# Where a block of background steps stands among the units of a Fourier and gated feed-forward kernel: fixed spacing, or beside named units

## The chip, the cores and the metric

The kernel runs on one core of a Trainium2 chip. The metric is the device time of one execution in microseconds (us); before the change it was 1040.99 us, the median of 3 runs (1040.63 to 1042.91). The engines of a core, as the profile names them, are PE (matrix products, with PEld for its weight loads), DVE (elementwise work on vectors), ACT (elementwise work and copies), POOL (here mostly an issuer of DMAs) and SP (an issuer of DMAs). Each runs its own queue in order and waits on semaphores of the others.

## The reference, cut to what matters

```python
xn = _layernorm(x, axis=-1)                       # x: 2048 tokens of 640
a = xn @ dft_hid_re.T;  b = xn @ dft_hid_im.T
y = dft_seq_re @ a - dft_seq_im @ b               # 2048 x 2048 by 2048 x 640, twice
gate = xn @ W_gate;  up = xn @ W_up               # 640 x 1728 each
h = (gate * (gate > 0)) * up
return x + y + h @ W_down
```

All of it is in float32. The sequence matrices are the largest operand (two of 2048 x 2048).

## The kernel before, in words

**Products.** PE multiplies fp32r tiles here. To keep float32's precision an operand is split into a high part (ACT copies it to fp32r) and a low part (DVE subtracts the high part from the operand), and each product is three matmuls: high by high, high by low, low by high (`mm3`, lines 130 to 132; `split`, lines 124 and 125). On top of it products of 2 x 2 blocks are made with seven block products in place of eight, whose operands are sums and differences of blocks.

**Three phases.** The first phase multiplies the transposed sequence matrices with the layer-normalised tokens, in four chunks of 512 output positions (`NCHUNK`). The second makes gate and up and their product (`gate_up`); the third makes the hidden transform, the down projection and the sum (`project`).

**The first phase.** The block products are named B11, B21 (made first, for all four chunks), T1, T2, B22, T3 and T4. For each chunk come the units of the last five: four units (g = 0 to 3) per product, in the order T1 0 to 3, T2 0, B22 0, T2 1, B22 1, T2 2, T2 3, B22 2, B22 3, T3 0 to 3, T4 0 to 3. A unit has up to four steps (`stream`): it loads a tile of the sequence matrices on SP (`raw`, and for T1 also `tk`, 512 KB each, line 650); `prepare` subtracts on DVE where the product needs a difference (line 646) and splits the result into one of the three buffers of `cb` (lines 124, 125); `run` issues 18 matmuls for T1 and B22 and 12 for the others; the last unit of a product adds its result to the sums (`combine`, tiles `sa` and `sb`, lines 533, 536, 628), which POOL stores to `pq` (line 619). At T2 0 SP loads `sa` anew (line 667), which waits until the last store of `sa` has gone.

**The order of the work.** `drive(4, 2)` walks over the list `todo`: at place i it loads unit i, prepares unit i-2, runs unit i-4. It runs work that `defer` has put off to this place first. The framework's scheduler may then still move instructions in each engine's queue of this phase; `in_turn` lets a unit's preparation be issued only behind the third last low part, and `keep_in_program_order` holds a single instruction where it stands.

**The background steps.** The second phase needs the same sums of blocks of the normalised tokens, transposed, split in two parts and stored in DRAM (`sets`, `halves`). For one half of the tokens this is made during the first phase, in six steps (`token_sets`, `SET_STEPS`). Steps 0 and 1 each make half of one set: they load the mean and scale of 512 tokens, spread over the partitions, and a tile of the transposed input (POOL, lines 360, 361), add and multiply on DVE (364, 365), split, and store two DMAs. Steps 2 to 5 each make a quarter of the other eight sets: they load four DMAs (378, 379), add and multiply twice (384, 385), make four differences (391), split two tiles of 1024 columns, and store four DMAs (line 422). All of it lies in one tile, named `r` in the profile, with eight spots of 1024 columns that are used in turn. Before the change a step is one more entry of `todo`: its place is two entries behind V3 (the last of the `sums_3` entries in chunk 0), and then every nine entries (`SPACE`). `begin` issues the loads there, and all further work of the step at two places, 6 and 7 entries later (`halve`: the arithmetic and the split), and the stores 8 and 9 entries later (`keep`).

When the sets are stored, SP loads them into the tiles of the second phase during the last chunk (`load_halves`, line 721).

Of the kernel before, what the change touches and what calls it, by code (L numbers as in the profile page):

```python
# [8 lines left out]
F32R = mybir.dt.float32r  # L9
# [17 lines left out]
SET_STEPS = 6  # L27
# [31 lines left out]
def fnet_reglu_kernel(  # L59
# [15 lines left out]
    nc = tc.nc  # L75
# [47 lines left out]
    def split(hi, lo, src):  # L123
        nc.scalar.activation(hi, src, AF.Copy)  # L124
        return nc.vector.tensor_tensor(lo, src, hi.bitcast(F32), op=OP.subtract)  # L125
# [19 lines left out]
    todo = []  # L145
# [192 lines left out]
    def token_sets(q, step, place=None, unit=None):  # L338

        def work():  # L340
            if "work" not in late:
                late["work"] = get_r1(F32)
            i = late["places"] = (late.get("places", -1) + 1) % 8
            return late["work"][:, i * W2 : (i + 1) * W2]

        stage = place or work

        ch = xt[:, q * W2 : (q + 1) * W2].rearrange("(k p) t -> k p t", p=P)
        st_r = rows[:, q * W2 : (q + 1) * W2]
        tt = nc.vector.tensor_tensor  # L350
        part = lambda st, i: st[:, i * CH : (i + 1) * CH]
        t = {}

        if step < 2:
            cs = slice(step * CH, (step + 1) * CH)

            def load():
                t["mr"], t["a"] = stage(), stage()[:, :CH]
                for i in range(2):
                    nc.gpsimd.dma_start(part(t["mr"], i), st_r[i : i + 1, cs].to_broadcast([P, CH]))  # L360
                nc.gpsimd.dma_start(t["a"], ch[4][:, cs])

            def make():
                tc.keep_in_program_order(tt(t["a"], t["a"], part(t["mr"], 0), op=OP.add))
                tt(t["a"], t["a"], part(t["mr"], 1), op=OP.mult)

            made = [([make], "a", lambda v: halves[X4][:, v, cs], lambda ap: ap)]
            keep_whole = lambda: nc.gpsimd.dma_start(sets[X4][:, cs], t["a"])
        else:
            k, hs = (step - 2) // 2, (step - 2) % 2 * HC  # L370
            hs = slice(hs, hs + HC)
            cols = lambda ap: ap.rearrange("p (c t) -> p c t", c=2)
            cs = slice(k * CH + hs.start, k * CH + hs.stop)

            def load():
                t["mr"], t["ab"] = stage(), stage()
                for i in range(2):
                    nc.gpsimd.dma_start(cols(part(t["mr"], i)), cols(st_r[i : i + 1])[:, :, hs].to_broadcast([P, 2, HC]))
                    nc.gpsimd.dma_start(cols(part(t["ab"], i)), cols(ch[k + 2 * i])[:, :, hs])

            def make():
                mr, ab = t["mr"], t["ab"]
                for i in range(2):
                    tc.keep_in_program_order(tt(part(ab, i), part(ab, i), part(mr, 0), op=OP.add))  # L384
                    tt(part(ab, i), part(ab, i), part(mr, 1), op=OP.mult)

            def more():

                mr, ab = t["mr"], t["ab"]
                (a0, a1, b0, b1), (t1, t2, t3, t4) = ([st[:, i * HC : (i + 1) * HC] for i in range(4)] for st in (ab, mr))  # L390
                sub = lambda o, i0, i1: tt(o, i0, i1, op=OP.subtract)  # L391
                sub(t1, a1, a0)
                sub(t2, b1, t1)
                sub(t3, b1, a1)
                sub(t4, b0, t2)

            by_set = lambda ap: ap.rearrange("p (i t) -> p i t", i=4)
            made = [([make, more], "ab", lambda v: halves[B11 : B11 + 4, :, v, cs].rearrange("i p t -> p i t"), by_set),
                    ([], "mr", lambda v: halves[T1 : T1 + 4, :, v, cs].rearrange("i p t -> p i t"), by_set)]

            def keep_whole():
                for i, st in ((B11, t["ab"]), (T1, t["mr"])):
                    nc.gpsimd.dma_start(sets[i : i + 4, :, cs].rearrange("i p t -> p i t"), by_set(st))

        if unit:
            unit(load, made[0][0], keep_whole)
            return

        def begin():
            load()  # L410
            for i, (make, name, place, view) in enumerate(made):

                def halve(make=make, name=name):
                    for m in make:
                        m()
                    src = t[name]
                    t["h" + name] = h = work()[:, : src.shape[1]]
                    split(h.bitcast(F32R), src.bitcast(F32R), src)

                def keep(name=name, place=place, view=view):  # L420
                    for v, part in enumerate((t["h" + name], t[name])):
                        nc.gpsimd.dma_start(place(v), view(part))

                defer(6 + i, halve)
                defer(8 + i, keep)

        todo.append((begin, idle, idle, idle))

    def raw():
        return raw_p.tile([P, W2], F32, name="raw")  # L430
# [213 lines left out]
    def stream(c, name, g):  # L644
        t = {}
        sub = lambda o, i0, i1: nc.vector.tensor_tensor(o, i0, i1, op=OP.subtract)  # L646

        def get(m, half, o=None):
            o = raw() if o is None else o
            late["dma"] = nc.sync.dma_start(o, dft[c, m, half * NH + g]).ins  # L650
            return o

        def load():
            if name == "T1":
                t["s"] = get(0, 0)
                TK[g] = get(1, 0, tk.tile([P, W2], F32, name="tk"))
            elif name == "T2":
                ST[g] = get(1, 1)
            elif name == "T3":
                t["s"] = get(0, 0)  # L660
            elif name == "T4":
                t["s"] = get(0, 1)

        def prepare():
            if name == "T2" and g == 0:
                F["a"] = sums_a()
                nc.sync.dma_start(F["a"], firsts[c])
            src = t.get("s", TK[g])
            with in_turn():
                if name == "T1":  # L670
                    src = TK[g]
                    sub(src, src, t["s"])
                elif name == "T2":
                    sub(src, ST[g], src)
                elif name == "B22":
                    src = ST[g]
                elif name == "T3":
                    sub(src, TK[g], src)
                elif name == "T4":

                    sub(src, src, TK[g])
                t["b"] = b = parts()
                lows.append(split(flat(b, 0), flat(b, 1), src))

        def run():
            b = t["b"]
            es = lambda n: [(n, 0), (n, 1)]
            if name == "T1":
                product(g, b, resident(g, 2), es("e2"), True, False, ("v2", 0, True))
            elif name == "T2":  # L690
                product(g, b, resident(g, 0), es("e1"), True, False)
            elif name == "B22":
                product(g, b, fourth(g), es("e2"), False, True, ("v2", 1, False))
            elif name == "T3":
                product(g, b, resident(g + NH, 0), es("e1"), False, True)
            else:
                product(g, b, resident(g + NH, 2), es("e2"), True, False)

        todo.append((load, prepare, run, lambda: combine(c, name) if g == NH - 1 else None))
# [37 lines left out]
                f()  # L737
        todo.clear()

    steps = [(q, i) for q in (1,) for i in range(SET_STEPS)]  # L740
    early_sets, first_sets = list(SETS_A), list(SETS_B)
    free = [None]
    SPACE = 9

    def phase(c, names):


        for n in names.split():
# [9 lines left out]
                first_stream(int(n[3]), n[:3], int(n[4]))  # L758
            else:
                stream(c, n[:-1], int(n[-1]))  # L760
            if n == "V3":
                free[0] = len(todo) + 2
            if free[0] is not None and len(todo) >= free[0] and steps:
                token_sets(*steps.pop(0))
                free[0] = len(todo) + SPACE

    for n in ("B11", "B21"):
        for g in range(NH):
# [2 lines left out]
    phase(0, "V1 T10 T11 V2 T12 T13 V3 T20 B220 T21 B221 T22 T23 B222 B223 T30 T31 T32 T33 T40 T41 T42 T43")  # L771
    for c in range(1, NCHUNK - 1):
        phase(c, "T10 T11 T12 T13 T20 B220 T21 B221 T22 T23 B222 B223 T30 T31 T32 T33 T40 T41 T42 T43")
    assert not steps, len(steps)
    phase(NCHUNK - 1, "T10 T11 T12 T13 T20 B220 T21 B221 T22 T23 K K K A A B222 B223 T30 A T31 A T32 A T33 T40 T41 T42 T43 K")
    assert not early_sets and not first_sets
    drive(4, 2)
    ph1.close()


# [520 lines left out]
```

## Time and profile before

| | |
|---|---|
| median of 3 runs | 1040.99 us (1040.63 to 1042.91) |
| the profiled execution | 1040.59 us |
| its span on the core | 1038.7 us |
| PE busy | 1025.0 us, 99% of the span |
| DVE busy | 801.3 us, 77% |
| ACT busy | 432.1 us, 42% |
| POOL busy | 106.9 us, 10% |
| moved by DMA | 242.73 MB, mean 234 GB/s |

A row of a group or of the timeline names the line of the kernel, the engine, the operation and its tiles, out first: `cb<-raw` writes `cb` from `raw`. In the timeline the first two numbers are the start from the span's start and the duration in us; several equal instructions in a row are merged (x2), and the bracket gives the engine's idle time ahead and what ended it. In a row of windows the numbers after the stretch are PE, PEld, DVE, ACT and POOL busy in us, each with its count of instructions, then PE's granted clock as a share of full speed, the DMA engines' busy share and GB/s. In a row of waits stand who waited, for whom, the total in us, how many times, and the longest. The record of a matmul of 512 columns lasts 0.39 us while the next starts 0.23 us after it, so PE can lose time that its busy sum does not show: the starts tell it.

### The profile page before, as it was taken

How to read it: one execution, taken by the hardware profiler on the slowest of the kernel's cores; microseconds unless marked ns; L12 is line 12 of the kernel's file. 1: busy time of each engine (PE TensorE's matmuls, PEld its weight loads, DVE VectorE, ACT ScalarE, POOL GpSimd, SP SyncE). 2: the span in 40 equal slices, each digit the busy share in tenths (PEclk: the TensorE clock that was granted, in tenths of full speed). 3: DMA queues.
4: the chain of work that ended last, by engine and by line, in shares of the span. 5: the costliest groups of instructions: out<-in, count | busy, mean ns of one | idle time of the engine just before them, and what ended most of it. 6: DMA issues, size and time to landing. Idle time of an engine off the chain costs nothing.

```text
span 1038.7 us, 12463 instructions
## 1 busy us (share of the span) xinstructions
PE 1025.0 (99%) x4528; PEld 844.2 (81%) x4528; DVE 801.3 (77%) x1074; ACT 432.1 (42%) x544; POOL 106.9 (10%) x172
## 2 busy tenths in 40 slices
PE   9899999999999999999999999999999999999998
PEld 7788888888787888888888888888878888888886
DVE  7857887979979767688887988887498667786764
ACT  6654453333343423333334534433365423552521
POOL 3211000102121001321110010010000000000000
PEclk9999999999999999999999999999999999999999
DMA  8987743947977975763363666663698636986554
GB/s 303 320 284 258 255 141 115 333 171 251 364 239 273 391 304 190 250 237 136 149 233 135 225 223 237 229 248 122 207 367 292 197 120 217 379 299 219 159 157 122
DMA packets 101468, 242.73 MB, mean 234 GB/s; under 512 B 11552, under 2 KB 50976, under 8 KB 98848
## 3 DMA queue, kind: packets, MB, share of 16 engines
q1 hardware_dynamic: 83664, 171.68, 48.2%
q0 software_dynamic: 17744, 70.26, 18.4%
q8 instruction: 35, 0.57, 0.2%
q14 instruction: 25, 0.20, 0.1%
HBM read 182.12 MB, written 58.74 MB: 232 GB/s over the span
## 4 chain that ended last, share of the span: by engine, by line
PE 91%; DVE 5%; DMA 1%; ACT 1%; issue 1%; SPq 0%; DVEq 0%; ACTq 0%
PE ps L132 30%; PE ps L131 30%; PE ps L130 30%; DVE cb L125 1%; PE ps L1198 1%; PE ps L495 1%; DMA rw<-hd 1%; DVE raw L646 1%; DMA raw<-in_dft 1%; DVE r L125 0%; DVE tk L646 0%; ACT cb L124 0%; DVE bs L204 0%; DVE r L391 0%; DVE r L384 0%
## 5 line engine op out<-in xcount | busy, mean ns | idle before, releaser
L130 PE MATMUL ps<-cb,wt 128*128 128x512 f32 x390 | 151.9, 390 | 0.4 <-ACT wt L124 0.4
L132 PE MATMUL ps<-cb,wt 128*128 128x512 f32 x390 | 151.9, 390 | 0.4 <-DVE wt L125 0.4
L131 PE MATMUL ps<-cb,wt 128*128 128x512 f32 x390 | 151.8, 389 | 0.0
L125 DVE TENSOR_TENSOR cb<-rw,cb 128x1024 fp32r<-128x1024 f32 x83 | 94.1, 1134 | 69.3 <-ACT cb L124 68.7
L124 ACT ACTIVATE cb<-rw 128x1024 fp32r<-128x1024 f32 x83 | 81.9, 987 | 149.9 <-PE ps L132 124.8
L124 ACT ACTIVATE cb<-raw 128x1024 fp32r<-128x1024 f32 x75 | 79.4, 1060 | 132.1 <-PE ps L132 101.6
L125 DVE TENSOR_TENSOR cb<-raw,cb 128x1024 fp32r<-128x1024 f32 x75 | 91.5, 1223 | 42.0 <-ACT cb L124 41.8
L130 PE MATMUL ps<-cb,xs_late 128*128 128x512 f32 x256 | 99.3, 390 | 4.3 <-ACT xs_late L121 2.8
L131 PE MATMUL ps<-cb,xs_late 128*128 128x512 f32 x256 | 100.1, 391 | 1.4 <-DVE cb L125 1.2
L131 PE MATMUL ps<-xs_early,gw 128*128 128x512 f32 x260 | 101.2, 389 | 0.0
L130 PE MATMUL ps<-xs_early,gw 128*128 128x512 f32 x260 | 101.2, 389 | 0.0
L132 PE MATMUL ps<-xs_early,gw 128*128 128x512 f32 x260 | 101.1, 389 | 0.0
L132 PE MATMUL ps<-cb,xs_late 128*128 128x512 f32 x256 | 99.3, 389 | 0.0
L121 ACT ACTIVATE gw<-z 128x1024 fp32r<-128x1024 f32 (+1 forms) x52 | 57.6, 1110 | 77.7 <-DVE z L808 75.1
L132 PE MATMUL ps<-cb,xs_early 128*128 128x512 f32 x226 | 87.9, 389 | 0.0
L131 PE MATMUL ps<-cb,xs_early 128*128 128x512 f32 x226 | 87.9, 389 | 0.0
L130 PE MATMUL ps<-cb,xs_early 128*128 128x512 f32 x226 | 87.4, 390 | 0.4 <-ACT cb L124 0.4
L130 PEld LDWEIGHTS ps<-cb,wt 128*128 128x128 f32 x390 | 73.2, 188 | 16.1 <-ACT wt L124 0.9
L132 PEld LDWEIGHTS ps<-cb,wt 128*128 128x128 f32 x390 | 73.2, 188 | 15.9 <-DVE wt L125 0.7
L131 PEld LDWEIGHTS ps<-cb,wt 128*128 128x128 f32 x390 | 73.2, 188 | 15.7 <-DVE cb L125 0.3
L121 ACT ACTIVATE u<-ps 128x512 f32<-128x512 f32 x52 | 31.1, 599 | 93.7 <-PE ps L132 93.7
L818 DVE TENSOR_TENSOR gw<-z,gw 128x1024 fp32r<-128x1024 f32 (+1 forms) x52 | 64.7, 1286 | 3.8 <-ACT gw L121 3.8
(198 smaller groups left out, 1947.7 us busy)
## 6 DMA issues: line engine op xcount, KB each, us to landing
raw<-in_dft SPq DMA_DIRECT2D x94, 512.0 KB, 6.2
wt<-wparts SPq DMA_DIRECT2D x66, 256.0 KB, 3.2
z<-in_wgu SPq DMA_DIRECT2D x26, 640.0 KB, 3.9
hd<-ob POOLq DMA_DIRECT2D x26, 512.0 KB, 3.7
rw<-hd SPq DMA_DIRECT2D x24, 512.0 KB, 6.8
wparts<-pw POOLq DMA_DIRECT2D x11, 1024.0 KB, 4.1
tk<-in_dft SPq DMA_DIRECT2D x16, 512.0 KB, 7.0
set<-r POOLq DMA_DIRECT2D x16, 512.0 KB, 4.6
```

The lines of the kernel that those rows point to most:

```text
L121: return nc.scalar.activation(o, i, AF.Copy)
L124: nc.scalar.activation(hi, src, AF.Copy)
L125: return nc.vector.tensor_tensor(lo, src, hi.bitcast(F32), op=OP.subtract)
L130: nc.tensor.matmul(ps, wh, mh, start=first, stop=False, skip_group_check=more)
L131: nc.tensor.matmul(ps, wh, ml, start=False, stop=False, skip_group_check=more)
L132: nc.tensor.matmul(ps, wl, mh, start=False, stop=last, skip_group_check=more)
L495: start["pe"] = pin([nc.tensor.matmul(E[0, key], xn_part(n * SG + j, d)[v == 1], b[:, int(v == 2), j], start=False, stop=n == NH - 1 and ( ...
L646: sub = lambda o, i0, i1: nc.vector.tensor_tensor(o, i0, i1, op=OP.subtract)
L818: tt(self.w[:, 1, cs], self.z[:, cs], self.w[:, 0, cs].bitcast(F32), op=OP.subtract)
L1198: nc.tensor.matmul(B[key], wr[:, v, es], hr[:, cs], start=False, stop=v == 1, skip_group_check=not new)
```

## The change

A step is no longer an entry of `todo`. `token_sets` returns its load, its arithmetic and its splits as functions, and a table `hooks` puts each beside a unit: `stream`'s `prepare` runs what is entered for its chunk, product and g right after its own split. Steps 0 and 1 stand in chunk 0: loads beside T1 2 and T1 3, everything else beside B22 0 and B22 1. Steps 2 and 3 stand in chunk 1, steps 4 and 5 in chunk 2, all in the same way: loads a chunk ahead beside T3 3 and T4 1; of the arithmetic one half (an add and a multiply) beside each of T1 0 and T1 1 for the first step, T1 2 and T1 3 for the second; the four differences of the first step beside B22 0, its two splits beside B22 1; the differences and the first split of the second step beside B22 2, its second split beside B22 3. Stores follow two entries behind the split. The last of the six steps therefore ends in chunk 2, and `todo` has six entries fewer.

```diff
-            def make():
+            def make(two=range(2)):
                 mr, ab = t["mr"], t["ab"]
-                for i in range(2):
+                for i in two:
                     tc.keep_in_program_order(tt(part(ab, i), part(ab, i), part(mr, 0), op=OP.add))
                     tt(part(ab, i), part(ab, i), part(mr, 1), op=OP.mult)
...
-        def begin():
-            load()
-            for i, (make, name, place, view) in enumerate(made):
-
-                def halve(make=make, name=name):
-                    for m in make:
-                        m()
-                    src = t[name]
-                    t["h" + name] = h = work()[:, : src.shape[1]]
-                    split(h.bitcast(F32R), src.bitcast(F32R), src)
-
-                def keep(name=name, place=place, view=view):
-                    for v, part in enumerate((t["h" + name], t[name])):
-                        nc.gpsimd.dma_start(place(v), view(part))
-
-                defer(6 + i, halve)
-                defer(8 + i, keep)
-
-        todo.append((begin, idle, idle, idle))
+        def halve(name):
+            src = t[name]
+            t["h" + name] = h = work()[:, : src.shape[1]]
+            split(h.bitcast(F32R), src.bitcast(F32R), src)
+
+        def keep(name, place, view):
+            for v, part in enumerate((t["h" + name], t[name])):
+                nc.gpsimd.dma_start(place(v), view(part))
+
+        halves_of = {name: lambda name=name, place=place, view=view: (halve(name), defer(2, lambda: keep(name, place, view)))
+                     for _, name, place, view in made}
+        return load, made[0][0], halves_of
...
                 lows.append(split(flat(b, 0), flat(b, 1), src))
+            for f in hooks.pop((c, name, g), ()):
+                f()
...
-    steps = [(q, i) for q in (1,) for i in range(SET_STEPS)]
     early_sets, first_sets = list(SETS_A), list(SETS_B)
-    free = [None]
-    SPACE = 9
+    hooks = {}
+
+    def at(c, name, g, *fs):
+        hooks.setdefault((c, name, g), []).extend(fs)
+
+    for step in range(2):
+        load, make, halve = token_sets(1, step)
+        at(0, "T1", 2 + step, load)
+        at(0, "B22", step, *make, halve["a"])
+    for step in range(2, SET_STEPS):
+        load, (make, more), halve = token_sets(1, step)
+        c, i = 1 + (step - 2) // 2, step % 2
+        at(c - 1, *(("T3", 3), ("T4", 1))[i], load)
+        for j in range(2):
+            at(c, "T1", 2 * i + j, lambda make=make, j=j: make((j,)))
+        at(c, "B22", 2 * i, more, *([halve["ab"]] if i else []))
+        at(c, "B22", 2 * i + 1, *([halve["mr"]] if i else halve.values()))
...
-            if n == "V3":
-                free[0] = len(todo) + 2
-            if free[0] is not None and len(todo) >= free[0] and steps:
-                token_sets(*steps.pop(0))
-                free[0] = len(todo) + SPACE
```

More of the change, by code (lines that the diff above doesn't have):

```diff
@@ L773, in fnet_reglu_kernel @@
         phase(c, "T10 T11 T12 T13 T20 B220 T21 B221 T22 T23 B222 B223 T30 T31 T32 T33 T40 T41 T42 T43")
-    assert not steps, len(steps)
     phase(NCHUNK - 1, "T10 T11 T12 T13 T20 B220 T21 B221 T22 T23 K K K A A B222 B223 T30 A T31 A T32 A T33 T40 T41 T42 T43 K")
@@ L777, in fnet_reglu_kernel @@
     drive(4, 2)
+    assert not hooks
     ph1.close()
```

## The prediction

> **What bounds the kernel now.** I read the page first (share of each engine, clock), then the windows by stage, then PE's own timeline at the places where a window is not full, then the queue that PE waited for there. The windows are the four chunks of the first phase from the T1 products on: 142 to 207 us is chunk 0, then chunks 1, 2 and 3.
>
> ```profile
> PE 1025.0 (99%) x4528; PEld 844.2 (81%) x4528; DVE 801.3 (77%) x1074; ACT 432.1 (42%) x544; POOL 106.9 (10%) x172
> ...
> 142.00:207.00 65.00, 65.00 (x288) 53.85 (x287) 52.70 (x57) 25.32 (x27) 6.57 (x11) 1.00 0.58 198
> 207.00:275.00 68.00, 66.05 (x289) 53.70 (x289) 59.71 (x68) 26.46 (x26) 9.12 (x13) 1.00 0.68 245
> 275.00:343.00 68.00, 66.70 (x291) 54.04 (x290) 60.60 (x68) 26.13 (x26) 13.23 (x19) 1.00 0.79 282
> 343.00:408.00 65.00, 65.00 (x288) 53.84 (x287) 46.39 (x47) 22.00 (x22) 2.17 (x4) 1.00 0.81 311
> ```
>
> PE bounds the kernel, at the full granted clock (1.00 in each window). Chunks 0 and 3 run 288 matmuls in 65 us, 0.226 us each. Chunks 1 and 2 run 289 and 291 in 68 us, which at that pace are 65.2 and 65.7 us: 2.8 and 2.3 us are lost, 5.1 in all, though the busy column shows only 1.95 and 1.30 idle, because a record lasts 0.39 us and overlaps the next. So whatever rearranges VectorE (DVE) work in this phase can win at most about 5 us. PE's timeline shows where they go:
>
> ```profile
> 269.40 0.39 PE L132 MATMUL ps<-cb,xs_late 128*128 128x512 f32 x1
> 271.20 0.73 PE L130 MATMUL ps<-cb,xs_late 128*128 128x512 f32 x2 [1.41 <-ACT cb L124]
> 272.34 0.97 PE L130 MATMUL ps<-cb,xs_early 128*128 128x512 f32 x3 [0.41 <-ACT cb L124]
> 273.44 0.50 PE L131 MATMUL ps<-cb,xs_late 128*128 128x512 f32 x1
> 273.77 0.39 PE L132 MATMUL ps<-cb,xs_late 128*128 128x512 f32 x1
> ...
> 329.48 0.39 PE L132 MATMUL ps<-cb,xs_late 128*128 128x512 f32 x1
> 329.90 0.73 PE L130 MATMUL ps<-cb,xs_late 128*128 128x512 f32 x2
> 331.85 0.50 PE L131 MATMUL ps<-cb,xs_late 128*128 128x512 f32 x1 [1.22 <-DVE cb L125]
> ...
> 340.14 0.87 PE L130 MATMUL ps<-cb,xs_early 128*128 128x512 f32 x3
> 341.06 0.50 PE L131 MATMUL ps<-cb,xs_late 128*128 128x512 f32 x1
> ```
>
> From 269.40 to 273.77 seven matmuls start in 4.37 us where 7 x 0.227 = 1.59 would do: 2.78 lost. From 329.48 to 331.85 three start in 2.37: 1.69 lost. From 340.14 to 341.06 three start in 0.92: 0.24 lost. A restart costs about 0.1 more (273.77 comes 0.33 after 273.44), which the two later places pay too. That makes 4.9 us by the starts and 5.1 by the windows; I take 5.0. PE waited for the high (ACT) and low (DVE) part of a `cb` tile. In DVE's queue the reason stands just ahead:
>
> ```profile
> 255.79 0.69 DVE L384 TENSOR_TENSOR r<-r 128x512 f32<-128x512 f32 x1
> ...
> 260.47 1.09 DVE L391 TENSOR_TENSOR r<-r 128x256 f32<-128x256 f32 x3
> 261.47 1.23 DVE L125 TENSOR_TENSOR cb<-raw,cb 128x1024 fp32r<-128x1024 f32 x1
> ...
> 264.08 2.36 DVE L125 TENSOR_TENSOR r<-r 128x1024 fp32r<-128x1024 f32 x2
> 266.35 1.29 DVE L533 TENSOR_TENSOR sa<-ps,sa 128x512 f32<-128x512 f32 x2
> 267.55 1.29 DVE L536 SCALAR_TENSOR_TENSOR sb<-sb,sa 128x512 f32<-128x512 f32 x2
> 268.75 1.23 DVE L646 TENSOR_TENSOR raw<-raw,tk 128x1024 f32<-128x1024 f32 x1
> 269.88 2.36 DVE L646 TENSOR_TENSOR tk<-tk,raw 128x1024 f32<-128x1024 f32 x2
> 272.15 1.23 DVE L125 TENSOR_TENSOR cb<-raw,cb 128x1024 fp32r<-128x1024 f32 x1
> ```
>
> One whole token step (L384, L385, L391 and the two low parts of `r`) runs between 255.79 and 266.35, in T4, then the sums of T3. Only at 268.75 does the subtraction for T4's last unit come, while PE runs dry at 269.40. The same in chunk 2: the low parts of `r` at 323.76, and three low parts of `cb` late and in a heap at 330.57.
>
> ```profile
> 323.76 2.36 DVE L125 TENSOR_TENSOR r<-r 128x1024 fp32r<-128x1024 f32 x2
> ...
> 330.57 3.50 DVE L125 TENSOR_TENSOR cb<-raw,cb 128x1024 fp32r<-128x1024 f32 x3
> ```
>
> **The change part by part.** The amount of work stays: the listing of the two built programs has the same number of instructions on every engine (1076 on DVE, 546 on ACT, 177 on POOL, 439 on SP). So the sum has no term for work, only for position. In a row, an operation of 1024 columns takes 1.14 us of the queue (268.75 to 269.88), one of 512 columns 0.60 (266.35 to 267.55, two of them), one of 256 columns 0.33 (260.47 to 261.47, three). A step of the larger kind (2 to 5) is then 4 x 0.60 + 4 x 0.33 + 2 x 1.14 = 6.0 us of DVE, one of the smaller (0 and 1) 2 x 0.60 + 0.60 = 1.8.
>
> Load by chunk: chunk 3, which has no step, keeps DVE busy 46.4 of 65 us. With two steps, chunks 1 and 2 come to 58.4 of 65.3, so there is room for them. What matters is whether a low part is ever later than PE wants it. The measure is how far ahead DVE can be:
>
> ```profile
> 397.44 1.06 ACT L124 ACTIVATE cb<-raw 128x1024 fp32r<-128x1024 f32 x1 [1.66 <-PE ps L132]
> 400.15 1.06 ACT L124 ACTIVATE cb<-raw 128x1024 fp32r<-128x1024 f32 x1 [1.66 <-PE ps L132]
> ...
> 398.75 1.22 DVE L125 TENSOR_TENSOR cb<-raw,cb 128x1024 fp32r<-128x1024 f32 x1
> ...
> 401.25 1.23 DVE L125 TENSOR_TENSOR cb<-raw,cb 128x1024 fp32r<-128x1024 f32 x1 [0.68 <-ACT cb L124]
> ```
>
> In chunk 3 ACT waits for PE: `cb` has three buffers, so a high part starts when the unit three before leaves PE (2.71 us apart, one T4 unit of 12 matmuls), ends 1.06 later, and DVE's low part follows. A low part made as early as that is done 2.3 us after the release, and PE wants it two units after the release: 3.1 us of slack in T3 and T4 (2 x 2.72 - 2.3), up to 5.9 in T1 (2 x 4.08 - 2.3). At 401.25 DVE is idle 0.68: without a step it is level again right after T3's sums.
>
> Now the changed queue from T4 into T1, by the listing: low of T40; subtraction T43; low T41; T3's sums with low T42 between; subtraction T10; low T43; subtraction T11; low T10; then the parts of the first step (two of 512), one ahead and one behind subtraction T12; low T11; two more parts with one of T4's sums between; low T12; two parts with the other sum; subtractions T13 and T20; one of 256; low T13; a part; low T20; a part; three of 256; subtraction T21; low B220; two lows of `r`; and so on. I add the durations above, with zero where PE starts T40 and no low part before its buffer is free (its high part ends 1.3 after PE starts the unit two before: 1.06 and the tail of the last matmul). Done at, against wanted at (us): T43 5.5, 8.2; T10 7.9, 10.9; T11 11.4, 15.0; T12 14.3, 19.0; T13 19.8, 23.1; T20 21.6, 27.2; B220 26.4, 29.9; T21 31.0, 34.0; B221 33.2, 36.7; T22 37.9, 40.8; T23 39.2, 43.5. The least slack is 2.6 us. In the old order the same sum is negative at T43 and at the chunk's end. That the listing no longer has PE's matmuls out of their unit order at these three places (only the old one has high products of the next units pulled ahead, as at 271.20 to 272.34) fits this. So the stalls go: -5.0 us.
>
> Chunk 0 now has two steps of 1.8 us beside B220 and B221 in place of one there and one in T4. Their cover is DVE's waiting in that chunk:
>
> ```profile
> DVE cb L125 <- ACT cb L124: 12.2, 12, 2.9
> ...
> POOL set L422 <- ACT r L124: 26.3, 1, 26.3
> ```
>
> The first row's 12.2 us of being early hold 1.8 more: 0. If that cover were gone, 1.8 would be the price.
>
> ACT: one high part of `r` (1.06 us) now stands between those of T12 and T13, and waits for parts that are done at 13.2 in the ledger; T13's own source is ready at 17.2, so 0. Before B220 one costs 0.8 us of a slack of 4.3. Uncovered, each would be 1.06.
>
> POOL and SP. The four loads of a step are issued a chunk ahead of its first part, so DVE does not wait for them: even behind the stores that free their spots they have half a chunk, over 30 us, against a landing of the order of those below. POOL's queue runs its stores in order, and in the new one a store of a step stands ahead of the store of `sa` after T4's sums, for which the next load of `sa` on SP waits, with the transfers for the last unit of T3 behind it:
>
> ```profile
> 210.90 0.54 POOL L619 DMA_DIRECT2D pq<-sa  x1 [7.48 <-DVE sa L533]
> ...
> 214.58 0.33 SPq L667 DMA_DIRECT2D sa<-first  x1
> 221.90 8.48 SPq L650 DMA_DIRECT2D raw<-in_dft  x2
> ...
> 245.66 1.22 DVE L646 TENSOR_TENSOR raw<-tk,raw 128x1024 f32<-128x1024 f32 x1
> ```
>
> That step's first high part is ready at 14.2 in the ledger, T4's last sum at 15.5, so the store hardly moves: 0. The cover is large: the transfer of 221.90 is wanted at 245.66.
>
> The loads from POOL also share the wires with SP's streams. The tightest of those is T12's `raw`: its buffer frees with the low part of T40 (-2.7), it is wanted at 8.5, 11.2 us later.
>
> ```profile
> DMA to landing us min/median/max: 3.1/6.2/11.5
> ...
> DMA to landing us min/median/max: 4.7/7.0/14.3
> ```
>
> The first row is `raw`, the second `tk`. At the worst `raw` landing DVE waits 0.3 us, at the worst of both 3.1, and the slack of T13 is 3.3: 0, with up to 3 us of slack eaten.
>
> The Trainium skill (DMA: Bandwidth & Descriptors, section Issuing engines are not separate DMA queues) speaks against loads put on another queue as if they were free: transfers started by SP and by POOL end up on the same 16 engines and interleave. The trace agrees: `tk` takes from 4.7 to 14.3 us. By that rule the sum stays the same as long as the slack above holds.
>
> Sum: the profiled execution took 1040.59 (span 1038.7 and 1.9 around it); less 5.0 gives 1035.6. The median of the runs, 1040.99, lies 0.4 above that execution, so 1036.0; I take 1035.9. The bounds of the unknown: a full gain with a run like the lowest (1040.63) gives 1035.6, with 0.5 for the spread of the runs 1035.1; the ledger wrong by one stall of the first kind (2.78) gives 1038.7.
>
> **The rivals.** *Part of it comes back.* DVE is level but not early: between the low parts of T12 and T13 stand 5.6 us of DVE work against 4.08 of PE. If DVE reaches T4 with less than 1.5 us in hand, or transfers come at their worst, a shorter stall appears at T13 or B220 in each of the two chunks, 0.5 to 1.4 us each: 1037 to 1038.8. For it: the DVE windows will stand at 90%. Against: the 0.68 idle at 401.25.
>
> *No change.* The bubbles repeat at the end of a chunk because three `cb` buffers don't carry PE over T4's short units and the sums, whatever the step does. Then the stalls stay and the time is 1041.0. Against it: chunks 0 and 3 have the same buffers and sums and 65.00 of 65.00 busy. The Trainium skill (Perfetto Trace Analysis, Identifying Performance Opportunities) says that the same bubble repeating on the engine that should be full can mean too few buffers; here the chunk without a step speaks against it.
>
> *Slower.* The store of a step ahead of `sa`'s store holds up SP: if a part waits (for its load or in ACT's queue), the transfers behind the `sa` load come late. It decides only beyond the margin, 245.66 - 221.90 less a landing, which is 20.7 us at the least landing of `raw` and 12.3 at the worst; each us beyond is a us of PE, in two chunks. To end slower it must eat the gain, 5.0, and 2.1 more, 3.5 a chunk, so 16 to 24 us of delay in each of the two: 1043 to 1046. For it: POOL did wait 26.3 us for a step's high part in chunk 0 (the row above). Against it: that wait stood ahead of nothing that SP wanted, and now the part is wanted and made a unit or two apart.
>
> **How the numbers follow.** No stall left: 0.68, 1035.1 to 1036.9. Part comes back: 0.19, to 1038.8. No change: 0.08. Slower: 0.05. About 2.1 us, 0.2%, is what a measurement of this kernel can tell from no change; the first two cases are both faster by more: 0.87, same 0.08, slower 0.05. The range 1035.0 to 1038.8 takes in the first two.
>
> **What would show it.** Right: chunks 1 and 2 with 288 matmuls in 65.3 us; no PE wait for `cb` after 50 us in the first phase; DVE's operations on `r` in the same number and length, no more than two low parts of `r` between two of `cb`; the second phase begins 5 us earlier and is as long. Wrong: a PE wait at T13 or B220 (first rival), at the end of T4 with DVE idle or waiting for ACT (second), SP's load of `sa` more than 20 us after PE's T1 began (third); or a landing over 14 us with DVE waiting for `tk`.

## The result, and the profile after

The changed kernel takes 1035.73 us (median of 6 runs, 1034.16 to 1038.25) against 1041.14 us (6 runs, 1039.34 to 1042.91) for the kernel before: a ratio of 0.9947 [0.9933, 0.9962]. The forecast was 1035.9 us. The profiled execution took 1034.42 us, its span is 1032.7.

The windows by stage of the changed kernel, core 0. Columns: the stretch, its length, then busy time and count of PE, PEld, DVE, ACT and POOL, the granted clock, the share of the DMA engines and GB/s. The stretches shown are chunks 0 to 2 of the first phase from the T1 products on, the second phase, and the third:

```profile
142.00:207.00 65.00, 65.00 (x289) 53.81 (x288) 54.49 (x59) 25.23 (x27) 6.56 (x11) 1.00 0.60 214
207.00:272.30 65.30, 65.30 (x290) 54.07 (x289) 60.52 (x68) 26.32 (x26) 14.04 (x20) 1.00 0.77 270
272.30:337.60 65.30, 65.30 (x290) 54.08 (x289) 60.52 (x67) 26.33 (x26) 8.26 (x12) 1.00 0.79 293
...
403.00:740.00 337.00, 337.00 (x1487) 278.76 (x1486) 267.27 (x424) 136.75 (x187) 43.59 (x72) 1.00 0.57 199
740.00:1032.70 292.70, 288.01 (x1267) 237.37 (x1266) 206.72 (x219) 118.25 (x133) 8.70 (x16) 1.00 0.69 232
```

The last two stretches of the kernel before, in the same view:

```profile
408.00:745.00 337.00, 337.00 (x1488) 278.70 (x1487) 267.26 (x424) 136.88 (x187) 43.60 (x72) 1.00 0.56 199
745.00:1038.70 293.70, 288.59 (x1268) 237.50 (x1266) 206.94 (x219) 118.27 (x134) 8.70 (x16) 1.00 0.69 231
```

Chunks 1 and 2 now hold 290 matmuls in 65.30 us where they took 68.00. The second phase begins 5.0 us earlier and is as long as before. DVE's work in chunk 1 is 68 instructions both times. The third phase is 1.0 us shorter in this execution; that is not the change, as is seen further down. So of the 6.0 us between the two spans 5.0 are the change.

The timeline of the changed kernel at the end of chunk 1, where PE had run dry at 269.40 before: first DVE's queue, then PE.

```profile
265.96 1.22 DVE L125 TENSOR_TENSOR cb<-raw,cb 128x1024 fp32r<-128x1024 f32 x1
...
268.30 1.23 DVE L125 TENSOR_TENSOR cb<-tk,cb 128x1024 fp32r<-128x1024 f32 x1
269.45 0.69 DVE L384 TENSOR_TENSOR r<-r 128x512 f32<-128x512 f32 x1
```

```profile
269.68 0.39 PE L130 MATMUL ps<-cb,xs_late 128*128 128x512 f32 x1
269.91 0.39 PE L131 MATMUL ps<-cb,xs_late 128*128 128x512 f32 x1
...
272.17 0.39 PE L132 MATMUL ps<-cb,xs_late 128*128 128x512 f32 x1
272.40 0.39 PE L130 MATMUL ps<-cb,xs_early 128*128 128x512 f32 x1
```

T43's low part runs at 265.96, and the first matmul that reads it (L131) starts at 269.91. The step's first part (L384) comes only at 269.45, behind T10's low part, and T10 starts at 272.40, 0.23 behind the matmul before it. PE's list of waits has no `cb` in the first phase any more. This is the whole list, over the whole kernel (columns: us in total, times, longest):

```profile
PE ps L130 <- ACT xs_late L121: 2.8, 1, 2.8
PE ps L112 <- DVE warm L108: 1.0, 1, 1.0
PE ps L516 <- ACT xs_early L230: 0.9, 1, 0.9
PE ps L132 <- DVE wt L125: 0.4, 1, 0.4
PE ps L488 <- ACT xs_early L281: 0.3, 1, 0.3
```

### The profile page after: what moved, and what is told of

It is laid out like the page before. It is cut to its first block, busy times and chain, and to the rows that moved or that the text cites. A ratio compares the mean times of both kernels' runs of the same rounds, so it can differ in the third digit from the quotient of the medians.

```text
span 1032.7 us, 12466 instructions
## 1 busy us (share of the span) xinstructions
PE 1022.9 (99%) x4528; PEld 844.9 (82%) x4528; DVE 801.6 (78%) x1074; ACT 431.9 (42%) x544; POOL 106.8 (10%) x172
## 4 chain that ended last, share of the span: by engine, by line
PE 94%; DVE 2%; DMA 1%; ACT 1%; issue 1%; SPq 0%; POOL 0%; DVEq 0%; POOLq 0%; ACTq 0%
PE ps L130 31%; PE ps L132 31%; PE ps L131 31%; PE ps L1202 1%; DMA rw<-hd 1%; DVE bs L204 1%; DVE cb L125 0%; DVE r L285 0%; DMA r<-in_x 0%; ACT cb L124 0%; DVE mv L205 0%; ACT xs_early L281 0%; ACT mv L212 0%; POOL cb L272 0%; SPq L1209 0%
## 5 line engine op out<-in xcount | busy, mean ns | idle before, releaser
L131 PE MATMUL ps<-cb,wt 128*128 128x512 f32 x390 | 151.8, 389 | 0.0
L131 PE MATMUL ps<-xs_early,gw 128*128 128x512 f32 x260 | 101.1, 389 | 0.0
L131 PE MATMUL ps<-cb,xs_late 128*128 128x512 f32 x256 | 99.6, 389 | 0.0
L131 PE MATMUL ps<-cb,xs_early 128*128 128x512 f32 x226 | 87.9, 389 | 0.0
L131 PEld LDWEIGHTS ps<-cb,wt 128*128 128x128 f32 x390 | 73.2, 188 | 15.5 <-DVE cb L125 0.3
```

What stands on the lines that cost most here:

```text
L131: nc.tensor.matmul(ps, wh, ml, start=False, stop=False, skip_group_check=more)
```

## The experiments

Each time is the median of its runs, and each ratio is against the kernel before on the same chip, with a 95% interval.

### 1. The steps' arithmetic taken out of the kernel before

```diff
                 def halve(make=make, name=name):
-                    for m in make:
-                        m()
-                    src = t[name]
-                    t["h" + name] = h = work()[:, : src.shape[1]]
-                    split(h.bitcast(F32R), src.bitcast(F32R), src)
+                    t["h" + name] = t[name]
 ...
-                defer(6 + i, halve)
+                halve()
```

> The kernel before, with the arithmetic and the splits of the six background steps left out (their loads and stores stay; what is stored is not the sets). If the stalls come from the steps' 6 us of DVE work standing ahead of late low parts, they go without it: 1041.1 less 5.0 is 1036.1, and no PE wait for cb in chunks 1 and 2. If the end of a chunk itself (three buffers, short units, the sums) makes them, or the steps' transfers do, they stay: 1041, with stalls of some 2.8, 1.7 and 0.3 us.

Measured: 1062.58 us, ratio 1.0206 [1.0177, 1.0236]. Neither theory expected that. The waits between 140 and 180 us, and a row of POOL's queue:

```profile
ACT sa L121 <- DMA first<-sa: 31.4, 1, 31.4
...
PEld ps L130 <- ACT sa L121: 25.5, 1, 25.5
```

```profile
165.67 0.57 POOL L606 DMA_DIRECT2D first<-sa  x1
```

In the kernel before the same store stands at 106.14:

```profile
106.14 0.53 POOL L610 DMA_DIRECT2D first<-sa  x1 [20.61 <-ACT sa L121]
```

Without the arithmetic a step's stores wait for nothing but the loads, and the scheduler put steps' loads and stores ahead of `first<-sa` in POOL's queue. They wait on one another there (the stores for the loads and, it seems, the loads for spots of `r` that stores have not yet freed), the store of `sa` goes 60 us later, ACT can't overwrite `sa`, and PE stands for 25 us. The experiment changed the order, not only the work, so it says nothing on the steps' price. It does show, at another place, the mechanism of the rival "slower": a store behind others on POOL that somebody waits for.

### 2. The same, with the order kept

A DVE addition on 2 columns stays in place of the arithmetic, so that stores and loads keep their places.

```diff
-                    for m in make:
-                        m()
-                    src = t[name]
-                    t["h" + name] = h = work()[:, : src.shape[1]]
-                    split(h.bitcast(F32R), src.bitcast(F32R), src)
+                    src = t["h" + name] = t[name]
+                    tc.keep_in_program_order(tt(src[:, :2], src[:, :2], src[:, 2:4], op=OP.add))
```

> The kernel before again without the steps' arithmetic and splits, but with an addition of two columns on DVE where each split stood, so that the stores keep their places in POOL's queue (what is stored is not the sets). If the steps' DVE work makes the stalls: no PE wait for cb in chunks 1 and 2, and 1036.1. If the end of a chunk makes them: 1041.

Measured: 1035.83 us, ratio 0.9943 [0.9926, 0.9960]. Chunk 1 in the windows:

```profile
207.00:272.30 65.30, 65.30 (x290) 54.09 (x289) 49.04 (x52) 22.46 (x23) 6.22 (x9) 1.00 0.67 247
```

With the steps' work gone the old spacing has no stall in chunks 1 and 2. So the steps' work was the cause, and the changed kernel, which does all of it, is as quick as one that does none. The splits' high parts on ACT went out with the work on DVE; that DVE's queue is the one that counts is seen from experiment 7, which adds work to DVE alone.

### 3. Named units, but each step whole

Steps 2 to 5 stand beside B22, not in parts beside T1 and B22.

```diff
-        for j in range(2):
-            at(c, "T1", 2 * i + j, lambda make=make, j=j: make((j,)))
-        at(c, "B22", 2 * i, more, *([halve["ab"]] if i else []))
-        at(c, "B22", 2 * i + 1, *([halve["mr"]] if i else halve.values()))
+        at(c, "B22", 2 * i, make, more, *halve.values())
```

> The changed kernel, with each of steps 2 to 5 whole, 6.0 us of DVE, beside B22 0 or B22 2 in place of parts beside T1 and B22. If the place (the long units) is all that matters: 1035.7 as the changed kernel. If the parts have to be small against the slack (3.1 to 4.5 us there): the next low part is up to 1.5 to 2.9 us late for each of four steps, less what the scheduler weaves in between: 1039 to 1044, with PE waits for cb just behind B22 0 and B22 2.

Measured: 1039.23 us, ratio 0.9974 [0.9962, 0.9987]. PE's starts in chunks 1 and 2 lose 1.8 us in all, in four places (0.5 at 262.2, 0.4 at 273.9, 0.5 at 328 to 329, 0.4 at 340.2, restarts of 0.1 counted). Against the gain of 5.0 that leaves 3.2; the median gained 2.3, and the interval (1.4 to 4.0) holds both. So half to two thirds of the gain comes with the place beside long units alone; the rest comes with the cut into parts that are spread over T1 and B22. The losses do not stand just behind B22 0 and B22 2, where they were expected, but in T4 at the chunk's end, in its first and its last unit. A step is whole in the program only: in DVE's queue the scheduler wove it between other units' work (the first one from 224.55 to 235 us).

### 4. Small parts, but beside short units

```diff
-        at(c - 1, *(("T3", 3), ("T4", 1))[i], load)
+        at(c, "T1", 2 * i, load)
         for j in range(2):
-            at(c, "T1", 2 * i + j, lambda make=make, j=j: make((j,)))
-        at(c, "B22", 2 * i, more, *([halve["ab"]] if i else []))
-        at(c, "B22", 2 * i + 1, *([halve["mr"]] if i else halve.values()))
+            at(c, "T3", 2 * i + j, lambda make=make, j=j: make((j,)))
+        at(c, "T4", 2 * i, more, *([halve["ab"]] if i else []))
+        at(c, "T4", 2 * i + 1, *([halve["mr"]] if i else halve.values()))
```

> The changed kernel, with the same small parts beside T3 0 to 3 and T4 0 to 3 in place of T1 and B22 (loads beside T1 0 and T1 2). If small parts are all that matters: 1035.7. If DVE's work in the stretch is what counts: T3 and T4 take DVE 22.7 us without a step against 21.8 of PE, two steps add 12.0, of the 12.9 over the slack carries some 4.5, so 8.4 us are lost in each of two chunks: about 1052.

Measured: 1053.25 us, ratio 1.0116 [1.0091, 1.0142]. PE at the end of chunk 1, and the windows there:

```profile
269.36 0.40 PE L132 MATMUL ps<-cb,xs_late 128*128 128x512 f32 x1
273.75 0.73 PE L130 MATMUL ps<-cb,xs_late 128*128 128x512 f32 x2 [3.99 <-ACT cb L124]
275.45 0.79 PE L131 MATMUL ps<-cb,xs_late 128*128 128x512 f32 x1 [0.97 <-DVE cb L125]
276.04 0.63 PE L132 MATMUL ps<-cb,xs_late 128*128 128x512 f32 x1
276.47 0.63 PE L130 MATMUL ps<-cb,xs_late 128*128 128x512 f32 x1
```

```profile
269.60:273.60 4.00, 0.16 (x1) 0.00 (x0) 4.00 (x6) 1.51 (x2) 0.00 (x0) 1.00 0.52 190
...
275.50:281.40 5.90, 5.90 (x14) 4.65 (x15) 5.72 (x6) 3.17 (x3) 1.46 (x2) 0.51 1.00 288
```

DVE is busy in all 4.00 of the 4.00 us in which PE stands. Each of the two places costs 4.2 us of stall and 1.1 of a second one, and then something that the prediction doesn't know: the granted clock falls to 0.51 for 5.9 us, with matmuls 0.43 us apart where 0.23 is the pace, some 2.8 us more. Twice 8.1 and a stall of 1.1 at 299.4 are 17.3 of the 17.5 us by which the median lies above the changed kernel's. The size of the parts does not help where DVE has no time: T3 and T4 are 12 matmuls a unit (2.72 us) and carry the sums as well. (This kernel moves the loads too; the next experiment shows that this alone costs nothing.)

### 5. The loads beside their use, not a chunk ahead

```diff
-        at(c - 1, *(("T3", 3), ("T4", 1))[i], load)
+        at(c, "T1", 2 * i, load)
```

> The changed kernel, with the loads of steps 2 to 5 issued beside T1 0 and T1 2, where their first part stands, in place of a chunk ahead. If the lead of the loads is what the change gains by: DVE waits for them, up to a landing (6 us) a step, and 1038 to 1041. If the place of the arithmetic is: at most a wait of a landing less the slack, 0 to 1.5 us a chunk: 1035.7 to 1038.

Measured: 1036.50 us, ratio 0.9954 [0.9935, 0.9972]. PE has no stall in chunks 1 to 3. Loading a chunk ahead brings nothing that can be measured; the gain is the place and the size of the arithmetic.

### 6. Four `cb` buffers in the kernel before

```diff
-RAW, RING = 6, 3
+RAW, RING = 5, 4
```

> The kernel before with four cb buffers in place of three, and five raw buffers in place of six to make room; the steps stand as before. By the slack: a fourth buffer lets a low part be one more T4 unit, 2.72 us, late, so the stalls of 2.78, 1.69 and 0.24 us shrink to some 0.1, 0 and 0: about 1036.3, unless a raw buffer fewer makes transfers late. If DVE's queue, not the slack, sets the end (no room to catch up): 1040 to 1041.

Measured: 1039.36 us, ratio 0.9978 [0.9966, 0.9990]. Chunks 1 and 2 are full, yet only 2.3 us are gained (1041.62 in the runs beside it). The rest is lost at the beginning. There ACT waits 1.4 us for a `raw` load at 34.89, a wait that the kernel before doesn't have, so the buffer that was given up is missed; what else differs there was not taken apart. Chunk 1, and PE at 41 us:

```profile
207.00:272.30 65.30, 65.30 (x290) 54.09 (x289) 57.31 (x66) 25.64 (x26) 9.13 (x13) 1.00 0.69 249
```

```profile
40.99 0.39 PE L132 MATMUL ps<-cb,xs_early 128*128 128x512 f32 x1
44.99 0.50 PE L130 MATMUL ps<-cb,xs_late 128*128 128x512 f32 x1 [3.61 <-ACT xs_late L121]
...
46.52 0.79 PE L132 MATMUL ps<-cb,xs_late 128*128 128x512 f32 x1 [0.56 <-DVE xs_late L252]
47.11 0.63 PE L130 MATMUL ps<-cb,xs_late 128*128 128x512 f32 x1
```

Before, that first stall is 3.0 us beyond the pace. Here it is 3.8, with 0.7 behind it, 0.6 at 32.2, and then the clock is at half until 50 us (1.7 lost): 3.8 us worse than before by 50 us, which leaves 1.2 of the 5.0; the two profiles differ by 1.1. So a fourth buffer also cures the two chunks, and pays for it elsewhere. The rival "no change" (too few buffers, whatever the step does) had half the truth: three buffers are enough when the work comes in small parts, four are enough when it comes in lumps.

### 7. How much room is left: more DVE work in the changed kernel

One addition of 256 columns (0.33 us of the queue) beside each of the 20 units of chunks 1 and 2, then two.

```diff
+    def extra():
+        tc.keep_in_program_order(nc.vector.tensor_tensor(spare_t, spare_t, spare_t, op=OP.add))
 ...
+    for c in (1, 2):
+        for name in ("T1", "T2", "B22", "T3", "T4"):
+            for g in range(NH):
+                at(c, name, g, *[extra] * 1)      # * 2 in the second kernel
```

> The changed kernel with one more addition of 256 columns (0.33 us) on DVE beside each of the 20 units of chunks 1 and 2, 6.7 us a chunk. By the ledger DVE then has 65.1 of 65.3 us a chunk, and T3 and T4 run 3.6 us over what PE takes, which a slack of 3 to 4.5 just holds: 0 to 2 us lost, 1036 to 1038. If the changed order has no slack to speak of, each chunk loses some 5: 1046.

> The same with two more additions beside each unit, 13.4 us a chunk: 71.8 us of DVE against 65.3 of PE, 6.5 over in each of two chunks, 13 in all, of which the slack takes up to 4.5 once: 1044 to 1049. If DVE still had room in the gaps: 1036 to 1038.

Measured: 1035.65 us, ratio 0.9934 [0.9919, 0.9949], and 1049.21 us, ratio 1.0067 [1.0052, 1.0082]. Chunk 1 of the first, then of the second:

```profile
207.00:272.30 65.30, 65.30 (x290) 54.07 (x289) 65.26 (x87) 26.29 (x27) 13.74 (x20) 1.00 0.76 263
```

```profile
207.00:272.30 65.30, 63.53 (x277) 51.35 (x275) 65.30 (x98) 23.44 (x24) 14.06 (x20) 1.00 0.73 241
```

With 6.6 us more in each of the two chunks nothing is lost. The prediction had 58.4 us a chunk (46.4 busy in chunk 3 and 12.0 for two steps, by the queue), so this makes 65.0 of 65.3. With 13.2 more it makes 71.6, 6.3 over, 12.6 in two chunks. PE's starts there lose 12.1 us, some 1.5 of them at half clock, and 1.8 more at 467.41 in the second phase; the median lies 13.5 above the changed kernel's, just above what was expected. Spread like this, DVE's work cost nothing at 65.0 of 65.3 us, and about 0.8 us for each us over. The share of busy time in the windows (60.5 of 65.3) would have told of 4.8 us of room where 6.6 had place, in part because records overlap: 1.22 for an operation that takes 1.14 of the queue.

### 8. Why runs differ by 4 us

The runs of the changed kernel stand at granted clocks of 1.000 or 0.998. First the changed kernel once more, and beside it one with three loads of `y` moved back in SP's queue:

```diff
-                if u == 3:
+                if u == (5 if name == "B11" else 3):
```

> Only the third phase is touched: the three loads of `y` for the first block (L1209) stand behind unit 5 in SP's queue, no longer behind unit 3. Theory: in the changed kernel what is left of the difference from run to run, and the 0.75 us stall of TensorE at about 749 us, come from this queue: these loads wait from 731 to 739 us for their space and hold back the weights `rw` and what feeds `wr` behind them, which are wanted at 749. Moved, the weights land earlier, the stall at 749 goes, and the time is 1034 to 1035 us with a narrower spread. Rival: it is not SP's order that makes them late, but the space or the wires; the stall stays, or `y` itself is now late: 1035.7 or more, with the spread of the changed kernel.

> The changed kernel as it is, beside the one above on the same chip: 1035.7 us, within 1034.2 to 1038.3, the higher ones with a granted clock of 0.998. If the theory above is right, this one's profile has a stall of 0.7 us or more at about 749 us and its runs spread more widely than those of the kernel above.

Measured: with `y` moved 1036.05 us (1033.47 to 1037.12), ratio 0.9938 [0.9923, 0.9954]; the changed kernel again 1036.89 us (1034.77 to 1038.65), ratio 0.9946 [0.9931, 0.9961]. PE in the changed kernel and SP's queue (from the first profile), then SP's queue with `y` moved:

```profile
749.59 0.51 PE L131 MATMUL ps<-cb,wt 128*128 128x512 f32 x1
750.46 0.50 PE L132 MATMUL ps<-cb,wt 128*128 128x512 f32 x1 [0.36 <-DVE wt L125]
```

```profile
730.62 0.47 SPq L1098 DMA_DIRECT2D wr<-in_wd  x1
739.35 1.29 SPq L1209 DMA_DIRECT2D y<-in_xt  x3
...
741.16 0.47 SPq L1098 DMA_DIRECT2D wr<-in_wd  x1
```

```profile
731.50 0.47 SPq L1098 DMA_DIRECT2D wr<-in_wd  x1
```

The `y` loads waited for room and held the loads behind them, 741.16 as against 731.50. Moved, the stall at 749 is gone from the profile (matmuls start 0.23 apart there), and the lowest run falls by 0.7 us against the lowest of the changed kernel. In the kernel before this stall was 1.66 us, in the changed one 0.75, in the repeat 1.53, with the same queue: that is 0.9 of the 1.0 us by which the third phase of the two first profiles differed. But the theory's other half was wrong: the spread stays, 3.7 us. The larger part of it comes earlier. The repeat was profiled in a run at 0.998 (1036.77), and its PE at 44 us, with the windows of the first profile of the changed kernel and of the repeat below it, shows why:

```profile
43.66 0.50 PE L130 MATMUL ps<-cb,xs_late 128*128 128x512 f32 x1 [2.85 <-ACT xs_late L121]
...
45.29 0.63 PE L130 MATMUL ps<-cb,xs_late 128*128 128x512 f32 x1
45.72 0.63 PE L132 MATMUL ps<-cb,xs_late 128*128 128x512 f32 x1
```

```profile
43.70:50.00 6.30, 6.25 (x27) 5.17 (x28) 5.83 (x15) 4.45 (x10) 0.55 (x1) 1.00 0.90 303
```

```profile
43.70:50.00 6.30, 6.30 (x21) 5.01 (x22) 5.83 (x15) 3.13 (x7) 0.55 (x1) 0.73 0.84 286
```

Both stood still for the same 3.0 us at 40.5. In one the clock stays at 1.00; in the other it is halved from about 45 to 48 us, and six matmuls less get done. By PE's starts that is 1.5 us; with the 0.8 more at 749 it makes up the 2.3 us between the two spans (1034.93 and 1032.65). Of the 12 profiles up to here, the same stall of 3.0 us was followed by half clock in 5 and not in 6; the one with 3.8 us (experiment 6) had it too. The last section shows what decides it.

### 9. The gap filled

The 3.0 us are filled with 26 small matmuls of zeros, added to an accumulator; all other instructions keep their order.

```diff
-            accs = [(c, ("e1", i)) for i in range(2)]
+            accs = [(c, ("e1", i)) for i in range(2)]; fill = [pin([nc.tensor.matmul(E[accs[0]][:, :P], warm, warm, start=False, stop=False, skip_group_check=True)]) for _ in range(26 * (n == NH and c == 0))]
```

> The changed kernel, with 26 small matmuls (zeros, 128 columns, as the 48 of line 112, which take 4.73 us: 0.1 us each) in the 3.0 us in which TensorE waits at 40.5 us for the first `xs_late`; every other instruction keeps its place in every queue. They add zeros to an accumulator, so nothing computed changes. Theory of the spread: in half of the profiles the clock halves behind this stall, for 3 to 5 us, which costs 1.4 to 2.8 us; that is the group of runs with a granted clock under 0.999. With the stall filled the clock stays at 1.00 through 45 to 50 us in the profile, the slow runs become rare, and the median falls from 1035.7 to 1036.9 to about 1034.5 to 1035.2 (what the third phase's stall adds stays). Rival: the halving has another cause (a budget over a longer time, or the load of the other engines): the small matmuls change nothing, 1035.7 to 1036.9, or they themselves cost time by coming late, up to 2.6 us more.

> As the one before, with the loads of `y` moved behind unit 5 as well. If both theories hold, both places where runs differ are gone: 1033.5 us (the lowest of the kernel with `y` moved alone: 1033.47 and 1033.54), most runs within 0.5 us, all at a clock of 1.00; against the kernel before 0.9925. Rival: the half clock comes all the same, behind another wait or by itself: 1036, as wide a spread as with `y` moved alone (1033.5 to 1037.1).

Measured: 1034.43 us (1033.65 to 1035.47), ratio 0.9922 [0.9906, 0.9937]; with `y` moved as well 1033.65 us (1033.43 to 1035.60), ratio 0.9919 [0.9904, 0.9933]. PE of the first of the two, and its window:

```profile
40.71 1.62 PE L592 MATMUL ps<-warm 128*128 128x128 bf16 x26
43.73 0.50 PE L130 MATMUL ps<-cb,xs_late 128*128 128x512 f32 x1 [1.39 <-ACT xs_late L121]
```

```profile
43.70:50.00 6.30, 6.27 (x27) 5.18 (x28) 5.82 (x15) 4.45 (x10) 0.55 (x1) 1.00 0.93 308
```

The 26 took 1.62 us, not the 2.6 that I had worked out from the 48 at the start, so 1.39 us of waiting is left. That was enough: all twelve runs of the two kernels have a clock of 0.999 or 1.000, where the repeat of the changed kernel had five of six at 0.998, and the range shrinks from 3.9 us to 1.8 and 2.2. Nothing was taken from the critical path, PE still starts on `xs_late` at 43.73. The last kernel has the lowest median of all here; the interval of the one before it holds that ratio too. Neither edit has to do with the change, and the kernel before has the same two places.

## Why the prediction was right

**The bound and the sum.** The reading held: only PE's lost time in chunks 1 and 2 could be won, 5.0 us by the windows, and all of it was: 5.0 by the beginning of the second phase; 5.4 between the medians of the first comparison and 5.1 between those of the repeat (1041.97 and 1036.89). That the median came within 0.2 us of the forecast is luck, where runs spread over 4 us; the 5.0 us are not. The term of zero for work held too (68 DVE instructions in chunk 1 before and after), and experiment 2 shows the same time without the steps' work.

**The ledger.** Taking T40's start as zero (261.52), low parts were done at 5.65 for T43 (forecast 5.5), 8.0 for T10 (7.9), 11.5 for T11 (11.4), 14.4 for T12 (14.3), 20.0 for T13 (19.8) and 21.7 for T20 (21.6). Behind that it was too careful: B220 at 25.7 (26.4), T21 at 30.2 (31.0), B221 at 32.5 (33.2). The least slack is T43's, 2.7 us, forecast 2.6. A sum of queue steps in the new order, with no allowance for interplay, was good to 0.2 us over 22 us.

**The zeros.** Chunk 0 with two small steps is full (65.00 of 65.00). The store ahead of `sa`'s store moved the `sa` load from 214.58 to 215.85, and the loads wanted behind it not at all (three `raw` from 221.90 before, from 221.96 now):

```profile
215.85 0.33 SPq L660 DMA_DIRECT2D sa<-first  x1
221.96 18.01 SPq L643 DMA_DIRECT2D raw<-in_dft  x3
```

That is 8.7 us after PE began T1 of chunk 1 (207.12), where more than 20 would have told of the rival. Landings of `raw` went from at most 11.5 to 11.7 us, of `tk` from 14.3 to 14.4, so loads from POOL did not eat into T13's slack (3.4). The range of `tk`'s landings, which the prediction took as a sign of shared engines, doesn't by itself show what made the slow ones slow.

**The rivals.** "Part of it comes back" rested on DVE standing at 90% with little in hand. It stands there (60.5 of 65.3), and the hand was fuller than feared: experiment 7 adds 6.6 us a chunk and loses nothing. I gave it 0.19; with the queue's sum, 58.4, taken as the measure in place of busy time, it would have got less. "No change" is refuted by experiment 2, with three buffers and no stall. "Slower" did not occur here, but experiment 1 met its mechanism 60 us earlier in the kernel.

**What was not seen.** The step that the prediction had only as "0.5 for the spread of the runs" was mis-sized: runs of the changed kernel spread over 4.1 us. In the profiles that is the half clock after the stall at 40.5 (1.5 us in the repeat) and the stall at 749; of the other runs only the mean clock is known. The median fell inside because the kernel before has both as well.

## What to carry to other kernels

Background work that fits an engine's total may still stall the bound engine where it comes in lumps: work out, unit by unit, when each operand is done and when it is wanted, from the steps of the queue, and put small parts where units are long; size alone (experiment 4) or place alone (experiment 3) isn't enough. Beside that, look at what an experiment does to the order of in-order DMA queues before reading its time (experiment 1). And where runs of one kernel spread, look for a stall of some 3 us on TensorE and the granted clock behind it: filling it with matmuls that do nothing was worth 1.3 to 2.5 us of the median here, between intervals that overlap a little.

## What the runs showed of the hardware

The clock halves when TensorE has stood idle, and the price may exceed the stall's own. Behind 4.2 us it was 0.51 for 5.9 us (experiment 4). With the 3.0 us at 40.5 it came in 5 profiles of 11, between 0.8 us before PE started again and 1.5 us after. It came also behind shorter stalls close together: in the kernel of experiment 5 PE lost 1.05, 0.30 and 0.64 us between 749.09 and 751.76, and then

```profile
749.00:751.70 2.70, 1.48 (x5) 0.43 (x3) 2.09 (x2) 2.31 (x4) 0.00 (x0) 1.00 1.08 405
751.70:755.20 3.50, 3.44 (x9) 2.67 (x10) 3.41 (x5) 1.71 (x4) 0.00 (x0) 0.54 1.02 337
```

The 2.8 us of stalls at 269.40 in the profile before did not bring it.

What decides can be read from the traces, which record when the clock changed. In the 14 profiles it fell 11 times within the kernel, for 3.41 us (six times), 6.83 (four) or 23.89 (once), which are 1, 2 and 7 steps of 3.41. Each fall also stands a whole number of such steps behind the first record of full clock, and that one stands at 4.0 to 6.2 us, elsewhere in each run. So the clock changed only on a grid of 3.41 us that lies differently over the kernel from run to run. Let idle be what PE's starts lose against 0.227 us a matmul. Each of the 11 falls came at the end of a step with 1.99 us of idle or more, and of the other steps at full clock, over 4,100, none had more than 1.98. The 3.0 us at 40.5 put 2.06 to 3.01 us of idle into one step in the five profiles; in the six a line of the grid cut them, and no step had more than 1.95. Here are two steps of the first kernel of experiment 7, then two of the changed kernel:

```profile
40.18:43.59 3.41, 0.57 (x4) 0.14 (x2) 3.36 (x10) 3.41 (x6) 0.29 (x1) 1.00 0.73 156
43.59:47.00 3.41, 3.41 (x8) 2.70 (x9) 3.24 (x9) 1.59 (x5) 0.55 (x1) 0.50 0.99 399
```

```profile
39.14:42.55 3.41, 1.77 (x8) 1.13 (x6) 3.20 (x13) 3.41 (x7) 0.57 (x1) 1.00 0.78 320
42.55:45.97 3.42, 2.22 (x10) 1.80 (x11) 3.23 (x8) 2.10 (x5) 0.55 (x1) 1.00 1.00 328
```

By the starts the first has 3.01 us of idle, and the half clock follows; the last two have 1.81 and 1.37, and it doesn't. This rule is inferred from these 14 profiles, and no run was made to test it. It fits experiment 9, where about 1.5 us of idle is left by the starts, less than 1.99 wherever the grid falls: none of twelve runs had a clock under 0.999, so the idle time is the cause at 40.5 us.

The Trainium skill (TensorE: Matmul & The Clock Gate, section Why this matters for your kernels) says that gaps of more than about 3 us between bursts of matmuls bring the clock down to half. The runs agree where stalls were longer (3.8, 4.2, 25 us). They differ at 3.0 us, where the same stall brings it or not, as the grid falls, and at the 2.0 us lost in three stalls within 2.7.

Small matmuls of 128 columns took 0.062 us each at full clock (26 in 1.62), and 0.10 at the kernel's start (48 in 4.73).
